# The end of a dense mixture layer: last unit's sums on VectorE, transposes in pairs, raw weights one by one

## The chip, the cores and the metric

The program runs on one core of a Trainium2 chip. The metric is the device time of one execution in microseconds (us), the median of several. The engines named here are TensorE (PE in the profile), VectorE (DVE), ScalarE (ACT), GpSimd (POOL) and SyncE (SP). Each works through its own instructions in order. Transfers are requested on the queues of SyncE and GpSimd.

## The reference, cut to what matters

Attention gives x, 1536 tokens of 512 values. A dense mixture layer follows, with eight experts that all see every token, and then a routed one, in which each token goes to one expert.

```python
def _moe_ref(x, w_gate, w1, w2):          # dense
    P = ...                               # 1536 x 8, normalised eight times
    out = np.zeros((N, D))
    for e in range(E):
        h = np.maximum(x @ w1[e], 0.0)
        out += P[:, e:e + 1] * (h @ w2[e])
    return out

def _moe2_ref(x, w_gate, w_output_gate, w1, w2):   # routed, x is the output above
    logits = x @ w_gate
    e_idx = np.argmax(logits, axis=1)
    gate_w = softmax(logits)[np.arange(N), e_idx]
    eom = 1.0 / (1.0 + np.exp(-(x @ w_output_gate)))
    for e in range(E):
        mask = e_idx == e
        h = np.maximum(x[mask] @ w1[e], 0.0)
        out[mask] = gate_w[mask, None] * eom[mask, e, None] * (h @ w2[e])
    return out
```

## The kernel before

Every float32 product is made of three matmuls of rounded parts (hi and lo): hi times hi, lo times hi, hi times lo. A raw weight tile is loaded, cast to hi on ScalarE (L481, L590) and subtracted to lo on VectorE (L482, L591).

The dense layer goes by half experts hx, 0 to 15. From hx 2 on its tokens are taken in sets of 512 (j), and each set of a half expert is a unit of Strassen's scheme: seven products s1 to s7 for the first layer of this unit, and between them seven products z1 to z7 for the second layer of the unit before. Their order is written out by hand:

```python
TURNS = "s1 z1 s2 z7 z6 s6 s7 z5 s5 z2 z4 s3 z3 s4".split()
```

Half experts up to 13 have three sets, 14 and 15 (the last expert) only two: these are the short ones, and the time in which weights have to be loaded and split is shorter there. The list `later` holds steps (a load, a sum, a split) of which one is taken between products. `load(which, hx, c)` requests one raw quarter of the weights of layer 1 or 2, on SyncE's or GpSimd's queue.

The second layer's results are collected in float32: ScalarE scales a product by the token's gate P (L862), and GpSimd's queue adds it to the sums in DRAM by an accumulating transfer (L867, x2d). `reload` fetches finished sums from x2d into the buffers `acc`.

The four token tiles 8 to 11 of the last expert are left for `rest()`, which ends the dense layer plainly, as half experts P = 16 and R = 17: `mm1_rest` makes the first layer in four blocks c of 12 matmuls of 128x512, `mm2` (in `tile_of`) the second layer for one token tile at a time. The z products of the last unit lie between P's blocks. `done(i)` says that tile i is final.

The routed layer starts inside this stage. `late_steps()` is a second sequence, of which a step is taken between the pieces of the dense one: for each final tile `flip` transposes it on TensorE (four transposes into a bank, a copy to r_xt on ScalarE), and `logits` multiplies it with r_w, the two gating weights side by side. `plain()` begins this phase. `choose`, `totals`, `ranks` and `place` find each token's expert and place, with many small operations on VectorE. The first eight tiles fill two early slots of 128 tokens (`early_*`), and the counts over all tiles (`final_*`) decide the rest. A slot's rows are fetched by an indirect transfer (xg), flipped (flip_x), and multiplied with its expert's weights (whi, wlo); between its two layers the result h is flipped too.

Of the kernel before, what the change touches and what calls it, by code (L numbers as in the profile page):

```python
# [387 lines left out]
class DenseMoe:  # L388
# [65 lines left out]
    def load(self, which, hx, c):  # L454
# [3 lines left out]
        if self.strassen(hx):  # L458
# [7 lines left out]
            (nc.sync if hx == self.FIRST or (which, hx) == (1, self.LAST) else nc.gpsimd).dma_start(  # L466
# [374 lines left out]
    def second(self, hx, j, h):  # L841
# [5 lines left out]
        v, o, *tq = (self.acc(i) for i in (0, 9, 1, 2, 10, 11))  # L847
        t, q = tq[2 * (u % 2):2 * (u % 2) + 2]
# [8 lines left out]
        def add(src, out, th, dh):  # L857

            for c in range(2):
                i = 4 * j + 2 * th + c  # L860
                s = slice(256 * c, 256 * c + 256)
                nc.scalar.activation(  # L862
                    out=out[:, s], in_=src[:, s], func=ACTF.Copy,
                    scale=self.P[:, i, hx // 2:hx // 2 + 1],
                )
# [57 lines left out]
    def steps(self, done, plain):  # L923
# [57 lines left out]
    def pieces(self, done, plain):  # L981
# [9 lines left out]
        waiting, behind = [], None  # L991

# [3 lines left out]
        def new_seconds(hx, n):  # L996
# [28 lines left out]
        for i, (hx, g) in enumerate(units):  # L1025
# [4 lines left out]
            if self.strassen(hx):  # L1030
                self.blocks = {}
                todo = {**self.first(hx, g), **(behind or {})}
                short = hx > self.FULL
                for k, turn in enumerate(self.TURNS):
# [15 lines left out]
                    elif last:  # L1050
                        for what in (self.FIRSTS_LATE if short else self.FIRSTS).get(turn, ()):
                            self.weights(1, n, what)
                    if last and turn == "s4":
                        self.later += [None] + loads(2, n)
                    if g == 0 and behind:
                        if short and turn == "z1":
                            new_seconds(hx, 2)
                        elif short and turn == "z3":
                            new_seconds(hx, 10)
                        elif not short and turn == "z6":  # L1060
                            new_seconds(hx, 0)
# [22 lines left out]
    def rest(self, u, behind, loads, done, plain):  # L1084
# [7 lines left out]
        h = {P: [self.hs[n] for n in (1, 2, 3, 5)], R: [self.hs[n] for n in (0, 4, 1, 2)]}  # L1092

# [7 lines left out]

        self.homes[8] = self.spare
        self.reload((8, 1, 2))
        for c in range(4):
# [151 lines left out]
class Routing:  # L1256
# [8 lines left out]
    def __init__(self, tc, keep, ident, ones, wg, wog, acc, x2d, x2e, psum):  # L1265
        self.tc, self.nc = tc, tc.nc
        self.ident, self.ones, self.acc, self.psum = ident, ones, acc, psum
        self.x2d, self.x2e = x2d, x2e
# [6 lines left out]
        for n, w in (("e", self.EARLY), ("f", self.NS - self.EARLY)):  # L1275
# [6 lines left out]
            })  # L1282
        self.fresh = keep.tile([1, self.NS], I32, name="r_fresh")
# [8 lines left out]
    def begin(self, pool):  # L1292
# [14 lines left out]
        def iota(n, step, base, mult, name):  # L1307
# [928 lines left out]
```

## Time and profile before

| what | value |
|---|---|
| median of 3 runs | 1314.18 us (1314.12 to 1314.45) |
| the profiled execution | 1316.05 us |
| its span on the core | 1314.3 us |
| PE busy | 1281.3 us, 97% |
| DVE busy | 879.2 us, 67% |
| ACT busy | 786.1 us, 60% |
| mean granted clock of TensorE | 0.992 of full |

The profile is of one execution. Its own time is 1.75 us above its span, which is what lies around the program on the core. Times of the trace are counted from the span's start. Attention takes about the first tenth, the dense layer goes on to about 1080 and the routed layer fills the rest.

### The profile page before, as it was taken

The numbers are of one execution on the slowest core, as the hardware profiler recorded it, in microseconds if no ns is written. First come the engines' busy times: TensorE is split into PE (matmuls) and PEld (weight loads), VectorE is DVE, ScalarE is ACT, GpSimd is POOL, SyncE is SP. The second block draws the span as 40 slices with busy tenths as digits, with TensorE's granted clock in tenths as the row PEclk, the third lists the DMA queues.
The fourth block names the chain that finished last, engine by engine and source line by source line (L and its number), as shares of the span: only waits on it lengthen the run. The fifth ranks groups of instructions, "written<-read, shape, count | busy, mean of one in ns | idle before, by whom it ended". The sixth has DMA issues, their size and how long they took to land. (4 is left out here: it accounts for less than half of the span.)

```text
span 1314.3 us, 27146 instructions
## 1 busy us (share of the span) xinstructions
PE 1281.3 (97%) x10227; PEld 1205.4 (92%) x10227; DVE 879.2 (67%) x1712; ACT 786.1 (60%) x1605; POOL 385.3 (29%) x398
## 2 busy tenths in 40 slices
PE   7999999999999999999999999999999998999998
PEld 7888889999999999999999999999999877787886
DVE  6854695877868778777778687787777448514252
ACT  4764322776767667767767676677666525324362
POOL 5652005233424233323334242333222301111110
PEclk8999999999999999999999999999999998999999
DMA  9850237788989798889788897889886668114360
GB/s 215 193 122 10 89 120 273 200 185 182 191 199 207 164 227 169 212 192 195 185 181 196 194 208 166 223 171 210 187 170 151 110 203 288 50 49 153 112 222 22
DMA packets 172828, 223.31 MB, mean 170 GB/s; under 512 B 48079, under 2 KB 102351, under 8 KB 172688
## 3 DMA queue, kind: packets, MB, share of 16 engines
q1 hardware_dynamic: 118448, 145.18, 36.1%
q0 software_dynamic: 54240, 76.30, 33.8%
q8 instruction: 83, 1.36, 0.4%
q14 instruction: 57, 0.47, 0.1%
HBM read 163.76 MB, written 58.46 MB: 169 GB/s over the span
## 5 line engine op out<-in xcount | busy, mean ns | idle before, releaser
L867 POOL DMA_DIRECT2D x2d<-acc x160 | 192.2, 1247 | 514.8 <-ACT acc L862 338.4
L703 PE MATMUL bank<-hi,hhi 128*128 128x256 f32 x748 | 211.5, 283 | 3.5 <-DVE acc L887 1.9
L703 PE MATMUL bank<-hi,hlo 128*128 128x256 f32 x748 | 211.7, 283 | 0.3 <-DVE hlo L738 0.3
L703 PE MATMUL bank<-lo,hhi 128*128 128x256 f32 x748 | 211.6, 283 | 0.0
L703 PE MATMUL bank<-Tlo,hi 128*128 128x256 f32 x640 | 181.0, 283 | 0.0
L703 PE MATMUL bank<-Thi,hi 128*128 128x256 f32 x640 | 180.3, 282 | 0.6 <-ACT t L783 0.6
L703 PE MATMUL bank<-Thi,lo 128*128 128x256 f32 x640 | 180.6, 282 | 0.0
L703 PE MATMUL bank<-hi,acc 128*128 128x256 f32 x744 | 148.0, 282 | 0.7 <-ACT acc L881 0.7
L703 PEld LDWEIGHTS bank<-hi,hhi 128*128 128x128 f32 x748 | 142.5, 190 | 4.4 <-DVE acc L887 2.1
L703 PEld LDWEIGHTS bank<-hi,hlo 128*128 128x128 f32 x748 | 142.1, 190 | 0.5 <-DVE hlo L738 0.5
L703 PEld LDWEIGHTS bank<-lo,hhi 128*128 128x128 f32 x748 | 142.0, 190 | 0.1
L703 PE MATMUL bank<-xhi,hi 128*128 128x256 f32 x480 | 135.4, 282 | 0.7 <-ACT t L797 0.7
L703 PE MATMUL bank<-xlo,hi 128*128 128x256 f32 x480 | 135.4, 282 | 0.0
L703 PE MATMUL bank<-xhi,lo 128*128 128x256 f32 x480 | 135.2, 282 | 0.0
L703 PEld LDWEIGHTS bank<-hi,acc 128*128 128x128 f32 x744 | 121.5, 190 | 0.9 <-ACT acc L881 0.9
L703 PEld LDWEIGHTS bank<-Thi,hi 128*128 128x128 f32 x640 | 121.0, 189 | 1.1 <-ACT t L783 1.0
L703 PEld LDWEIGHTS bank<-Thi,lo 128*128 128x128 f32 x640 | 120.7, 189 | 0.0
L703 PEld LDWEIGHTS bank<-Tlo,hi 128*128 128x128 f32 x640 | 120.3, 188 | 0.0
L738 DVE TENSOR_TENSOR hlo<-t,hhi 128x512 fp32r<-128x512 f32 x160 | 108.0, 687 | 14.5 <-ACT hhi L730 13.5
L730 ACT CAST hhi<-t 128x512 fp32r<-128x512 f32 x160 | 98.1, 621 | 27.4 <-DVE t L832 20.9
L862 ACT ACTIVATE acc<-acc,P 128x256 f32<-128x256 f32 x240 | 107.8, 504 | 5.1 <-DVE acc L904 3.5
L703 PE MATMUL bank<-lo,acc 128*128 128x256 f32 x372 | 105.1, 283 | 0.0
(312 smaller groups left out, 3254.6 us busy)
## 6 DMA issues: line engine op xcount, KB each, us to landing
x2d<-acc POOLq DMA_DIRECT2D x163, 256.0 KB, 5.4
Thi<-td SPq DMA_DIRECT2D x160, 256.0 KB, 3.6
Tlo<-td SPq DMA_DIRECT2D x160, 256.0 KB, 4.6
raw<-in_moe_w_dram POOLq DMA_DIRECT2D x100, 256.0 KB, 5.6
raw<-in_moe_w_dram SPq DMA_DIRECT2D x20, 1024.0 KB, 6.8
raw<-in_moe_w_dram SPq DMA_DIRECT2D x44, 256.0 KB, 4.3
vw<-in_v_dram SPq DMA_DIRECT2D x32, 120.0 KB, 3.6
kn<-in_k_dram SPq DMA_DIRECT2D x8, 384.0 KB, 5.9
```

What stands on the lines that cost most here:

```text
L703: self.nc.tensor.matmul(bank[:, 256 * f:256 * f + 256], x[:, o:o + 128], y[:, k], start=first and n == 1, stop=n == 12, skip_group_check=True,
L730: nc.scalar.copy(hi, src)
L738: nc.vector.tensor_tensor(out=lo, in0=src, in1=hi.bitcast(F32), op=ALU.subtract)
L862: nc.scalar.activation(out=out[:, s], in_=src[:, s], func=ACTF.Copy, scale=self.P[:, i, hx // 2:hx // 2 + 1],)
L867: nc.gpsimd.dma_start(out=self.sums[n:n + 256, 256 * dh:256 * dh + 256].rearrange("(c p) d -> p c d", p=128), in_=out.rearrange("p (c d) - ...
```

## The change

It has four parts. (1) Raw weights of half experts 14 and 15 are all requested on SyncE's queue, one at a time between products, where before most were requested on GpSimd's queue, four together. (2) The products of the last unit (15, second set) are added by VectorE, scaled by P, onto sums that `reload` has fetched into SBUF before; v, t and q live in buffers of T. (3) In `rest()` the last unit's z products and P's blocks lie in another order, the splits and loads around them too, and the first eight tiles are flipped in pairs into two copies (xts), ahead of P's last block. The index patterns are made by GpSimd first and cast by VectorE later (`begin_rest`). (4) x2e, the second scratch copy of the early tiles, is gone, and the steps of the routed layer have other distances.

```diff
@@ -463,7 +463,7 @@
...
-            (nc.sync if hx == self.FIRST or (which, hx) == (1, self.LAST) else nc.gpsimd).dma_start(
+            (nc.sync if hx == self.FIRST or hx > self.FULL else nc.gpsimd).dma_start(
@@ -844,8 +844,13 @@
...
-        v, o, *tq = (self.acc(i) for i in (0, 9, 1, 2, 10, 11))
-        t, q = tq[2 * (u % 2):2 * (u % 2) + 2]
+        final = u + 1 == len(self.sets)
+        if final:
+            v, t, q = (self.t_tile()[0].bitcast(F32) for _ in range(3))
+            o = None
+        else:
+            v, o, *tq = (self.acc(i) for i in (0, 9, 1, 2, 10, 11))
+            t, q = tq[2 * (u % 2):2 * (u % 2) + 2]
         bank = {}
 
@@ -856,6 +861,15 @@
...
 
+            if final:
+                for c in range(2):
+                    i = 4 * j + 2 * th + c
+                    a = self.acc(i)[:, 256 * dh:256 * dh + 256]
+                    nc.vector.scalar_tensor_tensor(
+                        out=a, in0=src[:, 256 * c:256 * c + 256],
+                        scalar=self.P[:, i, hx // 2:hx // 2 + 1], in1=a, op0=ALU.mult, op1=ALU.add,
+                    )
+                return
             for c in range(2):
@@ -938,9 +952,10 @@
...
 
     SECONDS_SOON = (
-        "B11", "sumT1", "sumT3", "T3", "sumT2", "T2", "sumT4", "T1", "B21", "T4", "B22",
+        "B11", None, "sumT1", None, "sumT3", None, "T3", None, "sumT2", 0, "T2", 1, "sumT4", None,
+        "T1", None, "B21", None, "T4", 2, "B22", None, 3,
     )
-    FIRSTS_LATE = {**FIRSTS, "s1": (), "s2": ("A11", "A12"), "z7": ("sumS1",)}
+    FIRSTS_LATE = {**FIRSTS, "s1": ("A11",), "z7": ("sumS1",)}
 
@@ -989,21 +1004,29 @@
...
 
-        def new_seconds(hx, n):
+        def new_seconds(hx):
 
             if hx <= self.FULL:
                 for what in self.SECONDS:
                     self.later += [partial(self.weights, 2, hx, what), None]
                 self.later += [None] + loads(1, hx + 1)
-            elif n == 2:
+            elif hx < self.LAST:
                 for what in self.SECONDS_SOON:
+                    if what is None:
+                        self.later.append(None)
+                    elif isinstance(what, int):
+                        self.later.append(partial(self.load, 1, hx + 1, what))
+                    else:
+                        self.later.append(partial(self.weights, 2, hx, what))
+            else:
+                for what in self.SECONDS:
                     self.later += [partial(self.weights, 2, hx, what), None]
-            elif n == 10:
-                self.later += loads(1, hx + 1)
+                self.later += [None] + loads(1, hx + 1)
 
@@ -1048,17 +1070,17 @@
...
                     elif last:
-                        for what in (self.FIRSTS_LATE if short else self.FIRSTS).get(turn, ()):
+                        for what in (self.FIRSTS_LATE if hx in soon else self.FIRSTS).get(turn, ()):
                             self.weights(1, n, what)
-                    if last and turn == "s4":
+                    if last and hx == self.FULL:
+                        for c in {"s5": (0,), "z3": (1, 2)}.get(turn, ()):
+                            self.load(2, n, c)
+                        if turn == "s4":
+                            self.later += [None, None, partial(self.load, 2, n, 3)]
+                    elif last and turn == "s4":
                         self.later += [None] + loads(2, n)
-                    if g == 0 and behind:
-                        if short and turn == "z1":
-                            new_seconds(hx, 2)
-                        elif short and turn == "z3":
-                            new_seconds(hx, 10)
-                        elif not short and turn == "z6":
-                            new_seconds(hx, 0)
+                    if g == 0 and behind and turn == ("z1" if hx in soon else "z6"):
+                        new_seconds(hx)
                 behind = self.second(hx, g, self.blocks)
                 continue
@@ -1090,6 +1112,10 @@
...
+        space = self.rpool.tile([128, 4, 768], F32, tag="xhi0", name="r_xts").rearrange(
+            "p k n -> p (k n)"
+        )
+        self.xts = [space[:, 512 * n:512 * n + 512] for n in range(2)]
@@ -1099,40 +1125,48 @@
...
+        def seconds(n):
+            for _ in range(n):
+                for _ in behind[order.pop(0)]():
+                    yield u
+
+        self.homes.update({i: self.acc(a) for i, a in ((4, 0), (5, 1), (6, 2), (7, 11))})
         self.homes[8] = self.spare
-        self.reload((8, 1, 2))
+        self.reload((4, 5, 6, 7, 8))
+        yield from seconds(1)
         for c in range(4):
             yield u
             for _ in self.mm1_rest(P, c, h[P][c]):
                 yield u
-            for turn in order[:(2, 3, 2, 0)[c]]:
-                for _ in behind[turn]():
-                    yield u
-            order = order[(2, 3, 2, 0)[c]:]
-            if c == 2:
-                for g in (1, 2):
-                    self.renew(g, F32)
-                self.later += [partial(self.split, 2, P, n) for n in range(4)]
-                self.later += [partial(self.reload, (10, 0, 3, 11, 9, 4, 5, 6, 7))] + loads(1, R)
-                self.later += [partial(done, i) for i in range(8)]
+            yield from seconds((2, 3, 1, 0)[c])
+            if c == 1:
+                a, b = (self.renew(g, F32) for g in (1, 2))
+                self.homes.update({0: a[:, 0], 1: a[:, 1], 2: a[:, 2], 3: b[:, 0]})
+                self.reload((0, 1, 2, 3, 9, 10))
+            elif c == 2:
+                for n in range(4):
+                    self.split(2, P, n)
+                    self.load(1, R, n)
                 plain()
+                for i in range(8):
+                    done(i)
         for t in range(4):
             for _ in tile_of(P, t):
                 yield u + 1
-            if t:
-                self.split(1, R, t - 1)
-                self.load(2, R, t - 1)
+            if t == 0:
+                self.homes.pop(7)
+                self.reload((11,))
+            self.split(1, R, t)
+            self.load(2, R, t)
         for c in range(4):
             yield u + 2
             for _ in self.mm1_rest(R, c, h[R][c]):
                 yield u + 2
-            if c == 0:
-                self.split(1, R, 3)
-                self.load(2, R, 3)
-            else:
-                self.split(2, R, c - 1)
-        self.split(2, R, 3)
-        done("x")
+            if c < 2:
+                self.split(2, R, 2 * c)
+                self.split(2, R, 2 * c + 1)
+            if c == 1:
+                done("x")
         for t in range(4):
@@ -1304,15 +1339,25 @@
...
+    def begin_rest(self):
+
+        pool = self.pool
+        nc, NT, NS, E = self.nc, self.NT, self.NS, self.E
+        for t, ti in self.made:
+            nc.vector.tensor_copy(t, ti)
 
         n = NS - self.EARLY
@@ -1341,25 +1383,26 @@
...
-        if i < self.TILES:
-            self.nc.sync.dma_start(out=self.x2e[rows, :], in_=self.acc(i))
-        else:
+        if i >= 4:
             self.nc.gpsimd.dma_start(out=self.x2d[rows, :], in_=self.acc(i))
...
-    def flip(self, i):
+    def flip(self, i, xt=None):
         nc = self.nc
         tr = self.psum("a", [128, 4, 128])
         x = self.acc(i)
         for k in range(4):
             nc.tensor.transpose(tr[:, k], x[:, 128 * k:128 * k + 128], self.ident)
-        xt = self.pool.tile([128, 4, 128], F32, tag="r_xt", name="r_xt", bufs=1)
+        if xt is None:
+            xt = self.pool.tile([128, 512], F32, tag="r_xt", name="r_xt", bufs=1)
+        xt = xt.rearrange("p (k n) -> p k n", k=4)
         nc.scalar.copy(xt, tr)
-        self.xt = xt
+        self.xt[i] = xt
 
     def logits(self, i):
         ps = self.psum("b", [128, 2 * self.E])
+        xt = self.xt.pop(i)
         for k in range(4):
-            self.nc.tensor.matmul(ps, self.xt[:, k], self.w[:, k], start=(k == 0), stop=(k == 3))
+            self.nc.tensor.matmul(ps, xt[:, k], self.w[:, k], start=(k == 0), stop=(k == 3))
         self.nc.vector.tensor_copy(self.lg[:, i], ps)
 
@@ -2012,7 +2054,7 @@
...
-        "routed": {"a": (4,), "b": (5,), "t": (0, 1), "m2": (3, 2), "m1": (6, 7)},
+        "routed": {"a": (4, 0), "b": (5,), "t": (0, 1), "m2": (3, 2), "m1": (6, 7)},
@@ -2125,8 +2167,7 @@
...
 
-            def tiles(i, n, first, w):
-                yield from wait(first)
@@ -2136,7 +2177,19 @@
...
-            yield from tiles(0, T, 4, 2)
+            while 0 not in finished:
+                yield
+            for j in range(T):
+                routing.flip(j, moe.xts[j % 2])
+                if j:
+                    routing.logits(j - 1)
+                if j % 2:
+                    yield
+                if j == 3:
+                    routing.begin_rest()
+            routing.logits(T - 1)
+            routing.choose(0, T)
+            yield from wait(6)
             routing.totals(T)
             routing.ranks(0, T)
```

What stands in each engine's order is shown at three places. The first is SyncE's queue at the end of the dense layer; `raw` from L471 are second-layer weights of P, `raw` from L474 first-layer weights of R, `acc` and `spare` fetched sums. Before:

```order
L657 DMA acc_107<-x2d 128x512 x2
L471 DMA raw<-in_moe_w_dram 128x512 x4
L1297 DMA r_w<-in_moe_w_gate_dram 128x4x8
L1297 DMA r_w<-in_moe_w_output_gate_dram 128x4x8
L657 DMA acc_110<-x2d 128x512
L657 DMA acc_107<-x2d 128x512
L657 DMA acc_13512<-x2d 128x512
L657 DMA acc_110<-x2d 128x512 x2
L657 DMA acc_13512<-x2d 128x512 x2
L657 DMA acc_13513<-x2d 128x512 x2
L474 DMA raw<-in_moe_w_dram 128x4x128 x4
```

With the change:

```order
L657 DMA acc_106<-x2d 128x512 x3
L657 DMA acc_109<-x2d 128x512
L657 DMA spare<-x2d 128x512
L471 DMA raw<-in_moe_w_dram 128x512 x4
L657 DMA acc_13485<-x2d 128x512 x3
L657 DMA acc_13486<-x2d 128x512
L657 DMA acc_109<-x2d 128x512 x2
L474 DMA raw<-in_moe_w_dram 128x4x128 x4
L1332 DMA r_w<-in_moe_w_gate_dram 128x4x8
L1332 DMA r_w<-in_moe_w_output_gate_dram 128x4x8
L657 DMA acc_109<-x2d 128x512
```

The two requests of r_w stood right behind P's raw weights; now they stand behind eleven fetched sums in all and behind R's four raw loads.

The second place is VectorE at the end of P's first layer; `lo` from L482 are the split parts of P's second-layer weights, `r_lg` (L1363, now L1406) the copies of the logits. Before:

```order
L689 SCALAR_TENSOR_TENSOR hlo<-bank_13460,hhi 128x512
L904 TENSOR_TENSOR acc_110<-bank_13390,acc_110 128x512
L1311 CAST r_ilo<-r_iota 128x128
L1311 CAST r_ihi<-r_iota 128x20
L1319 CAST r_ihalf<-r_ihi 1x18
...
L1311 CAST r_tok<-r_iota 128x12
L1311 CAST r_desc<-r_iota 128x8
...
L1340 MEMSET r_fresh 1x2
L482 TENSOR_TENSOR lo_13565<-raw,hi_13564 128x512
...
L482 TENSOR_TENSOR lo_13587<-raw,hi_13586 128x512
```

With the change (L868 is the addition of a product onto a fetched sum):

```order
L868 SCALAR_TENSOR_TENSOR acc_109<-Thi,P,acc_109 128x256
L689 SCALAR_TENSOR_TENSOR hlo<-bank_13493,hhi 128x512
L868 SCALAR_TENSOR_TENSOR acc_106<-bank_13355,P,acc_106 128x256 x2
L482 TENSOR_TENSOR lo_13525<-raw,hi_13524 128x512
...
L482 TENSOR_TENSOR lo_13543<-raw,hi_13542 128x512
L1406 COPY r_lg<-bank_13593 128x16
...
L1406 COPY r_lg<-bank_13621 128x16
L1360 CAST r_ilo<-r_iota 128x128
L1360 CAST r_ihi<-r_iota 128x20
```

The casts of the index patterns stood ahead of the four splits and now stand behind the first logits; the splits now stand directly behind the last unit's last sums.

The third place is TensorE at slot 0 of the routed layer: the matmuls of L1411, L1405 and L1406 (now L1454, L1448, L1449) form the totals and ranks of all tiles, L1886 (now L1929) flips h, and L1857 (now L1900) multiplies. Before:

```order
L1848 MATMUL bank_14252<-ident,xg 128x128 x4
L1362 MATMUL bank_14261<-r_w,r_xt 128x16 x4
L1886 MATMUL bank_14284<-ident,h 128x128 x4
L1886 MATMUL bank_14293<-ident,h 128x128 x4
L1857 MATMUL bank_14302<-whi_13558,ht0hi 128x512
...
L1857 MATMUL bank_14302<-whi_13558,ht0lo 128x512
L1411 MATMUL bank_14312<-r_run,ones 128x8
L1405 MATMUL bank_14314<-r_oh,r_upper 128x32
L1406 MATMUL bank_14314<-r_run,ones 128x32
L1857 MATMUL bank_14302<-whi_13558,ht0hi 128x512
```

With the change:

```order
L1900 MATMUL bank_14251<-wlo_13950,xthi 128x512
L1900 MATMUL bank_14251<-whi_13949,xtlo 128x512
L1454 MATMUL bank_14265<-r_run,ones 128x8
L1448 MATMUL bank_14267<-r_oh,r_upper 128x32
L1449 MATMUL bank_14267<-r_run,ones 128x32
L1891 MATMUL bank_14365<-ident,xg 128x128 x4
L1929 MATMUL bank_14374<-ident,h 128x128 x4
...
L1929 MATMUL bank_14383<-ident,h 128x128 x4
L1900 MATMUL bank_14392<-whi_13571,ht0hi 128x512
```

The totals stood behind both flips of h and nine matmuls of slot 0's second layer; now they stand ahead of both flips, and between them and the flips stands only the flip of the second slot's rows.

## Rows read from the trace of the kernel before

**Rows 1.** Table by stretches: us, busy PE, PEld, DVE, ACT, POOL, PEclk, DMA share, GB/s.

```profile
940.00:960.00 20.00, 19.07 (x158) 18.66 (x157) 15.34 (x25) 14.17 (x29) 6.09 (x7) 1.00 0.87 214
960.00:980.00 20.00, 18.07 (x146) 17.74 (x145) 15.73 (x26) 13.83 (x28) 3.57 (x4) 0.97 0.83 189
980.00:1000.00 20.00, 18.74 (x146) 18.33 (x145) 13.89 (x23) 11.42 (x24) 6.92 (x8) 0.94 0.83 174
...
1020.00:1040.00 20.00, 19.32 (x140) 18.15 (x139) 12.23 (x20) 11.88 (x24) 4.77 (x4) 1.00 0.71 131
1040.00:1060.00 20.00, 16.56 (x85) 13.83 (x84) 7.91 (x21) 7.37 (x16) 5.95 (x10) 0.91 0.76 151
...
1080.00:1100.00 20.00, 18.93 (x92) 15.21 (x91) 18.18 (x72) 8.09 (x13) 3.28 (x4) 1.00 0.63 216
1100.00:1120.00 20.00, 15.98 (x80) 13.59 (x80) 12.31 (x15) 10.86 (x14) 1.08 (x2) 0.83 0.85 296
1120.00:1140.00 20.00, 18.34 (x108) 15.23 (x106) 14.58 (x68) 9.02 (x16) 1.63 (x2) 1.00 0.04 15
...
1280.00:1300.00 20.00, 20.00 (x95) 16.34 (x94) 6.91 (x8) 8.04 (x12) 1.01 (x1) 1.00 0.05 18
```

**Rows 2.** Timeline of TensorE: start, duration, line, operation, count [idle before, releaser].

```profile
973.04 0.28 PE L703 MATMUL bank<-Thi,hi 128*128 128x256 f32 x1
...
974.48 0.28 PE L703 MATMUL bank<-hi,hhi 128*128 128x256 f32 x1
...
978.00 0.39 PE L703 MATMUL bank<-hi,hhi 128*128 128x256 f32 x1 [1.93 <-DVE acc L887]
...
1046.51 0.39 PE L682 MATMUL bank<-xhi,hi 128*128 128x512 f32 x1
...
1049.28 0.39 PE L631 MATMUL bank<-hi,hhi 128*128 128x512 f32 x1
...
1053.10 0.50 PE L631 MATMUL bank<-lo,hhi 128*128 128x512 f32 x1 [3.44 <-DVE lo L482]
...
1062.52 0.96 PE L1362 MATMUL bank<-r_w,r_xt 128*128 128x16 f32 x8
...
1063.33 0.64 PE L1354 MATMUL bank<-ident,acc 128*128 128x128 f32 x4
...
1063.72 0.48 PE L631 MATMUL bank<-hi,hhi 128*128 128x512 f32 x1
...
1109.00 1.89 PE L1362 MATMUL bank<-r_w,r_xt 128*128 128x16 f32 x8 [4.02 <-ACT r_xt L1356]
```

**Rows 3.** Timeline of ScalarE: casts of raw weights, dense (L590), then routed (L1821).

```profile
994.14 0.62 ACT L590 CAST hi<-raw 128x512 fp32r<-128x512 f32 x1 [3.15 <-DMA raw<-in_moe_w_dram]
...
1106.47 1.99 ACT L1821 CAST whi<-raw 128x1024 fp32r<-128x1024 f32 x2 [2.17 <-DMA raw<-in_moe_w_dram]
```

**Rows 4.** Timeline of GpSimd with its queue: raw loads of the last short expert.

```profile
988.09 3.36 POOL L466 DMA_DIRECT2D raw<-in_moe_w_dram  x4
```

**Rows 5.** Timeline of VectorE: around the split of P's weights, and the final routing chain.

```profile
1050.44 0.23 DVE L1311 CAST r_ilo<-r_iota 128x128 f32<-128x128 int32 x1 [4.47 <-POOL r_iota L1309]
...
1052.36 0.69 DVE L482 TENSOR_TENSOR lo<-raw,hi 128x512 fp32r<-128x512 f32 x1
...
1052.96 1.89 DVE L482 TENSOR_TENSOR lo<-raw,hi 128x512 fp32r<-128x512 f32 x3
...
1126.81 0.17 DVE L1466 TENSOR_SCALAR r_ni<-bank 128x8 int32<-128x8 f32 x1 [1.52 <-PE bank L1411]
...
1133.13 2.33 DVE L1824 TENSOR_TENSOR wlo<-raw,whi 128x1024 fp32r<-128x1024 f32 x2
```

**Rows 6.** Timeline of SyncE's queue: the two requests of the gating weights (r_w).

```profile
1036.58 0.43 SPq L1297 DMA_DIRECT2D r_w<-in_moe_w_gate_dram  x1
1037.06 0.50 SPq L1297 DMA_DIRECT2D r_w<-n_moe_w_output_gate_dram  x1
```

**Rows 7.** Line view of L1297, the same two requests: time to landing.

```profile
DMA to landing us min/median/max: 4.4/4.5/4.7
```

More of the change, by code (lines that the diff above doesn't have):

```diff
@@ L991, in pieces @@
         waiting, behind = [], None
+        soon = range(self.FULL + 1, self.LAST)
         def loads(which, hx):
             return [partial(self.load, which, hx, c) for c in range(4)]
-        def new_seconds(hx, n):
+        def new_seconds(hx):
             if hx <= self.FULL:
@@ L1032, in pieces @@
                 todo = {**self.first(hx, g), **(behind or {})}
-                short = hx > self.FULL
                 for k, turn in enumerate(self.TURNS):
@@ L1050, in pieces @@
                     elif last:
-                        for what in (self.FIRSTS_LATE if short else self.FIRSTS).get(turn, ()):
+                        for what in (self.FIRSTS_LATE if hx in soon else self.FIRSTS).get(turn, ()):
                             self.weights(1, n, what)
-                    if last and turn == "s4":
-                        self.later += [None] + loads(2, n)
-                    if g == 0 and behind:
-                        if short and turn == "z1":
-                            new_seconds(hx, 2)
-                        elif short and turn == "z3":
-                            new_seconds(hx, 10)
-                        elif not short and turn == "z6":
-                            new_seconds(hx, 0)
+                    if last and hx == self.FULL:
[4 more added lines that the diff above has]
+                    elif last and turn == "s4":
+                        self.later += [None] + loads(2, n)
+                    if g == 0 and behind and turn == ("z1" if hx in soon else "z6"):
+                        new_seconds(hx)
                 behind = self.second(hx, g, self.blocks)
@@ L1263, with __init__ @@
     EARLY, TILES = 2, 8
-    def __init__(self, tc, keep, ident, ones, wg, wog, acc, x2d, x2e, psum):
+    def __init__(self, tc, keep, ident, ones, wg, wog, acc, x2d, psum):
         self.tc, self.nc = tc, tc.nc
         self.ident, self.ones, self.acc, self.psum = ident, ones, acc, psum
-        self.x2d, self.x2e = x2d, x2e
+        self.x2d = x2d
         self.wg, self.wog = wg, wog
@@ L1282, in __init__ @@
             })
+        self.xt = {}
         self.fresh = keep.tile([1, self.NS], I32, name="r_fresh")
@@ L1305, in begin, with iota @@
         )
-        def iota(n, step, base, mult, name):
-            ti = pool.tile([128, 128], I32, tag="r_ohhi", name="r_iota", bufs=1)
-            nc.gpsimd.iota(ti[:, 0:n], pattern=[[step, n]], base=base, channel_multiplier=mult)
-            t = pool.tile([128, n], F32, name=name)
-            nc.vector.tensor_copy(t, ti[:, 0:n])
-            return t
-        self.i_lo = iota(128, 1, 0, 0, "r_ilo")
-        self.i_hi = iota(NS, 1, 0, 0, "r_ihi")
+        def iota(n, step, base, mult, name, tag):
+            ti = pool.tile([128, n], I32, tag=tag, name="r_iota", bufs=1)
+            nc.gpsimd.iota(ti, pattern=[[step, n]], base=base, channel_multiplier=mult)
+            return pool.tile([128, n], F32, name=name), ti
+        made = [
+            iota(128, 1, 0, 0, "r_ilo", "r_ohhi"), iota(NS, 1, 0, 0, "r_ihi", "r_le"),
+            iota(NT, 128, -2048, 1, "r_tok", "r_val"), iota(E, -1, E, 0, "r_desc", "r_ptg"),
+        ]
+        self.i_lo, self.i_hi, self.tok, self.desc = (t for t, _ in made)
+        self.lg = pool.tile([128, NT, 2 * E], F32, name="r_lg")
+        self.made = made
+    def begin_rest(self):
[3 more added lines that the diff above has]
+            nc.vector.tensor_copy(t, ti)
         n = NS - self.EARLY
@@ L1327, in begin @@
         )
-        self.tok = iota(NT, 128, -2048, 1, "r_tok")
-        self.desc = iota(E, -1, E, 0, "r_desc")
         self.unit = pool.tile([128, E], F32, name="r_unit")
         nc.vector.memset(self.unit, 1.0)
-        self.lg = pool.tile([128, NT, 2 * E], F32, name="r_lg")
         self.oh = pool.tile([128, NT, E], F32, name="r_oh")
@@ L1830, in gather @@
         self.nc.gpsimd.indirect_dma_start(
-            out=xg, out_offset=None, in_=self.r.x2e if s < self.r.EARLY else self.r.x2d,
+            out=xg, out_offset=None, in_=self.r.x2d,
             in_offset=bass.IndirectOffsetOnAxis(ap=self.r.of("gidx", s), axis=0),
@@ L2000 @@
     x2d = dram.tile([N, DM], F32, name="x2d")
-    x2e = dram.tile([128 * Routing.TILES, DM], F32, name="x2e")
     td = dram.tile([N // 512, 2, 4, 128, 512], F32, name="td")
@@ L2073 @@
         routing = Routing(
-            tc, const, ident, ones, moe2_w_gate, moe2_w_output_gate, acc, x2d, x2e, psum
+            tc, const, ident, ones, moe2_w_gate, moe2_w_output_gate, acc, x2d, psum
         )
@@ L2126, in wait, with tiles @@
                     yield
-            def tiles(i, n, first, w):
-                yield from wait(first)
+            def tiles(i, n, w):
                 for j in range(i, i + n):
@@ L2159, in late_steps @@
                 moe2.gather(s)
-            yield from wait(3)
             moe2.split(0, 1)
@@ L2163, in late_steps @@
             moe2.split(0, 1)
-            yield from wait(6)
+            yield from wait(4)
             moe2.flip_x(0)
-            yield from wait(3)
+            yield from wait(4)
             moe2.split(0, 1)
-            yield from wait(6)
+            yield from wait(5)
             moe2.split(0, 1)
             finished.add("early")
-            yield from tiles(T, NT - T, 0, 2)
+            yield from tiles(T, NT - T, 2)
             routing.totals(NT)
```

## The prediction

> **What bounds the kernel now.** I read the table by stretches first, then TensorE's timeline around each hole, then the other engines' timelines at the same moments. In the table [rows 1] the reader is to see that TensorE is full nearly everywhere (20.00 of 20 us in the last stretch shown) at granted clock 1.00, so a microsecond lost on TensorE moves the end by a microsecond. Holes stand only where the change works: the two short experts (940 to 1000) and the closing stage, from 1027 on. Idle time there is 20 minus PE's busy time: 0.93, 1.93 and 1.26 in the short experts, and 0.68, 3.44, 1.07, 4.02 and 1.66 in the five closing stretches shown. To that comes the low clock: a mean of 0.97 over 20 us is 1.2 us at the lower level (1.2 GHz for 2.4), which costs 0.6; 0.94 costs 1.2, 0.91 costs 1.8 and 0.83 costs 3.4. Together 5.9 us in the short experts and 16.1 in the closing stage. This is the lower figure. Counted from start to start of neighbouring matmuls, against the spacing of undisturbed ones, I get 7 and 18.8, because the matmuls beside a wait are stretched too (those at 978.00 and 1053.10 [rows 2]). I use 7.0 and 18.8: 25.8 us is all that this change can win.
>
> Who is late: in the short experts ScalarE, whose casts of raw weights wait up to 3.15 us for the transfer (994.14 [rows 3]). It was requested on GpSimd's queue, four pieces in one burst of 3.36 us starting at 988.09 [rows 4], behind the accumulating transfers of that queue. In the closing stage there are two large holes. The second layer's first matmul group waits 3.44 us at 1053.10 for its split weights (L482) [rows 2]; VectorE had waited 4.47 us for GpSimd's index pattern (r_iota) just ahead of them [rows 5]. And at 1109.00 the logits wait 4.02 us for a copy on ScalarE [rows 2], which there stood behind a cast of expert weights that had itself waited 2.17 us for its transfer (1106.47 [rows 3]).
>
> **The change part by part.**
>
> *Raw weights one by one on SyncE's queue.* They no longer stand behind accumulates, and are asked for up to ten microseconds earlier. All waits of the short experts should go: 7.0 gained, so the closing stage starts at T = 1027.3 - 7.0 = 1020.3. Bounds: 0 if SyncE's own fetches of T hold them as long, 7.0 if not; I take the upper end, since the slots in SyncE's order lie 3 us or more ahead of the casts. Every one of these requests now delays the T fetches behind it by about 0.4 us (by r_w's requests, the nearest row, 0.43 and 0.50 [rows 6]); these are asked for a product or more ahead and hide it.
>
> A sentence of the Trainium skill speaks against this part ("DMA: Bandwidth & Descriptors", section "Issuing engines are not separate DMA queues"): transfers of all issuers share the same sixteen engines, and spreading them over issuers saves only the time of issuing. By it alone the gain would be the few tenths by which one issue is shorter, and the whole sum 7 us worse. Rows 4 show why I don't follow it here: what is late is the request, not the transfer.
>
> *Last unit's products added on VectorE into sums fetched ahead.* It takes the accumulating transfers, their landing and the fetch behind them off the end of the unit. ScalarE's scalings go; VectorE gets two 128x256 additions a product. One product of 12 matmuls takes 1.44 us (973.04 to 974.48 [rows 2]), one of P's first-layer blocks 2.77 (1046.51 to 1049.28). Seven products and three blocks end at T + 10.1 + 8.3 = T + 18.4, and one product waits for a sum on VectorE, about 0.25 (bounds 0 and the 0.69 of one such VectorE operation [rows 5]). So T + 18.6.
>
> *Eight transposes in pairs, logits behind them.* TensorE does two flips (0.39 each with its gap, 1063.33 to 1063.72 [rows 2]) and then wants the first logits, at T + 19.3. They need r_w, the gating weights. The order shows r_w moved on SyncE: before it was requested right after P's raw weights, now behind R's four raw loads, each of which waits until VectorE has split the P weights (four L482). These stand behind the last sums: z3's two additions end at T + 19.6 (no row; between 0 and two times 0.6 after z3), then 0.69 and three more in 1.89 [rows 5], T + 22.1; the last raw load goes out in 0.4; r_w's two requests at T + 22.55 and 23.05 [rows 6] take 4.4 to 4.7 us to land [rows 7]: T + 27.4. TensorE idles from 19.3 to 27.4: **8.2 us**, and nothing covers it, because P's last block stands behind the logits in TensorE's order. Lower bound: if r_w were there, ScalarE's flip copy, behind four casts, would end near T + 20.8, a wait of 1.5.
>
> The Trainium skill puts the fixed cost of a transfer at about 2 us ("DMA: Bandwidth & Descriptors", section "Latency and other measured facts"). By it the hole would be 5.7 us rather than 8.2; r_w's own rows [rows 7] show more than twice that, and the measured value stands.
>
> *The clock behind the hole.* After an idle stretch the trace shows the lower level for a while: [rows 1] give 3.6 us of it in the stretch with the 3.44 idle, 6.8 us in the one with the 4.02. What follows here is light work, six flips, eight logits (0.81 each, 1062.52 to 1063.33; such a group of eight matmuls lasts 0.96 at the full clock and 1.89 at the lower, at 1109.00 [rows 2]) and one block: 2.3 + 6.5 + 2.8 = 11.6 us at full clock. Bounds: 1.8 (as after 3.44 idle) to 11.6 (all of it at half). I take 5.
>
> *Second layer of P.* Its fourth tile wants the bank that VectorE frees only behind the early routing chain, some 25 small operations (0.14 each, as in the next part) and one large, 4 us; most lies beside two tiles' matmuls, 1.15 stays (0 to 4). Four small waits (r_run, a flip's bank, the gathered rows, the first slot's split) are 0.2 to 0.7 each, together 1.6 (0 to 3).
>
> *Final counts ahead of the slot's flips.* In before the three small matmuls of the final totals stood nine matmuls into slot 0's second layer, so VectorE's chain lay beside matmuls. Now they stand ahead of the flips of h, and VectorE does the chain (46 small operations, 1126.81 to 1133.13, 6.3 us [rows 5]) ahead of the xtlo that frees the bank of the second h flip. TensorE has only two flips to do meanwhile: 6.3 + 0.6 + 0.3 - 0.7 = **6.5**, and some 0.1 for handing on: 6.6. Bounds: 4.5 if the chain packs tighter, 8.9 if the two wlo operations ahead of it (2.33 together [rows 5]) are not done. The clock behind it: 1.7 (0.8 to 3.4, [rows 1]).
>
> *Gone with it*: the iota wait, the ScalarE copy behind late expert loads (they are now requested earlier in the order, ahead of three of R's raw loads), the second scratch copy: all in the 18.8.
>
> **Sum.** Against the profiled execution's own 1316.05: -25.8 + 0.25 + 8.2 + 5.0 + 1.15 + 1.6 + 6.6 + 1.7 = -1.3, or 1314.8. The median of the runs is 1.87 below the profiled one, so 1313. By the lower figure of the gain, 22.0, it would be 1316.7 for the median.
>
> **Rivals.**
>
> A, the forecast: both new waits come as worked out and eat the gain. 1309 to 1317, by the bounds of the waits and of the clock.
>
> B, one of the two is not there: r_w lands before the flips (SyncE's raw loads don't wait as I read them), or VectorE's chain finishes under other work. For it: the waits are read from an order, and VectorE has room, with 7.91 and 12.31 us of work in the 20 us from 1040 and from 1100 [rows 1]. Against: both engines work in order. Without the r_w hole but with ScalarE's 1.5, 6.7 less, and the clock with it up to 5: 1301 to 1306. Without the chain's wait, 8.3 less: 1305.
>
> C, slower: the clock stays at the lower level through all of the flips and logits. It costs 11.6 instead of 5, 1320, and it decides as soon as more than 9 us of that stage run at half. For it: flips and logits are much lighter than the 128x512 groups that followed the holes of before. Against: in before the level came back within 7 us although flips and logits stood in it.
>
> D, the change doesn't do what it says in the short experts: SyncE, in order, holds raw loads behind T fetches that wait for a free buffer, and they land as late as before. Against: GpSimd's burst alone takes 3.36 us [rows 4]. Half to all of the 7 is missing: 1316 to 1320. The rule of the Trainium skill named above would end here too.
>
> **How the numbers follow.** A 45%, B 25%, C 20%, D 10%. The likeliest gives 1313. The bound of what can be told from no change is 0.2%, 2.6 us. Faster than 1311.6 takes a third of A and all of B: 0.40. Between 1311.6 and 1316.8 lies the larger part of A and half of D: 0.33. Slower: C, the other half of D and a little of A: 0.27. The range reaches from the middle of B to beyond C's centre, 1303 to 1321; A's own is 1309 to 1317.
>
> **What would show it.** In the profile after: no wait of ScalarE on raw between the short units; TensorE's first logits after the dense layer with 8 us of idle time ahead, released by the DMA of r_w; a granted clock well below 1 in the 12 us behind; a second wait of 6 to 7 us at the second flip of h, released by VectorE's xtlo; no wait on the P split or on r_xt. The forecast is wrong if r_w's request starts before T + 15, if the second h flip waits less than 3 us, or if the short experts keep more than 3 us of idle time.

## The result, and the profile after

| kernel | median | runs | ratio to the kernel before | TensorE's path | granted clock |
|---|---|---|---|---|---|
| before | 1314.15 us | 1311.67 to 1315.87 | | 1079.97 us | 0.992 |
| changed | 1325.55 us | 1324.19 to 1328.42 | 1.0092 [1.0078, 1.0107] | 1088.75 us | 0.979 |

The change costs 11.4 us; 1313 and a range of 1303 to 1321 were forecast. The last columns are of the profiled executions. "TensorE's path" is the time from the first matmul with T (the first Strassen unit) to the start of the last matmul. It leaves out the first 230 us, which differ by up to 4.4 us between executions (the first T matmul stands between 225.88 and 230.26 in the profiles shown here), and what follows the last matmul. Here and below a ratio compares the means of the runs, its bracket is a 95% interval, and one run of 3721 us (r_w early) is left out of it.

The table by stretches of the changed kernel, columns as in [rows 1]:

```profile
940.00:960.00 20.00, 20.00 (x170) 20.00 (x169) 17.84 (x30) 16.29 (x33) 4.87 (x5) 1.00 0.89 221
960.00:980.00 20.00, 20.00 (x169) 20.00 (x169) 16.91 (x28) 14.29 (x29) 4.83 (x4) 1.00 0.85 178
980.00:1000.00 20.00, 20.00 (x170) 20.00 (x169) 16.04 (x27) 15.49 (x31) 5.31 (x5) 1.00 0.82 184
...
1020.00:1040.00 20.00, 18.32 (x120) 16.45 (x118) 13.10 (x24) 7.99 (x15) 4.14 (x11) 1.00 0.84 235
1040.00:1060.00 20.00, 11.58 (x49) 10.81 (x50) 2.26 (x16) 1.76 (x3) 0.50 (x1) 0.57 0.33 97
1060.00:1080.00 20.00, 20.00 (x80) 17.80 (x81) 6.49 (x29) 4.77 (x10) 0.00 (x0) 0.58 0.07 18
1080.00:1100.00 20.00, 19.77 (x96) 16.06 (x94) 16.84 (x54) 8.24 (x12) 2.90 (x2) 1.00 0.64 225
...
1120.00:1140.00 20.00, 13.02 (x60) 10.41 (x59) 16.41 (x67) 7.99 (x13) 0.10 (x1) 0.74 0.16 53
```

The short experts (first three rows) have no idle time and the full clock; that is the gain that was forecast. From 1040 on stand two rows at a clock of 0.57 and 0.58, then one hole at 1120. TensorE's timeline shows the two places:

```profile
1037.29 1.04 PE L1394 MATMUL bank<-ident,acc 128*128 128x128 f32 x8
1048.42 1.86 PE L1405 MATMUL bank<-r_w,r_xts 128*128 128x16 f32 x8 [10.10 <-DMA r_w<-n_moe_w_output_gate_dram]
...
1071.99 0.77 PE L631 MATMUL bank<-hi,hhi 128*128 128x512 f32 x1
1072.56 0.63 PE L631 MATMUL bank<-lo,hhi 128*128 128x512 f32 x1
...
1076.83 0.47 PE L631 MATMUL bank<-hi,hlo 128*128 128x512 f32 x1
1077.13 0.39 PE L631 MATMUL bank<-hi,hhi 128*128 128x512 f32 x1
...
1122.13 0.36 PE L1454 MATMUL bank<-r_run,ones 128*128 128x8 f32 x2 [0.44 <-DVE r_run L1433]
...
1124.49 0.86 PE L1929 MATMUL bank<-ident,h 128*128 128x128 f32 x4 [1.06 <-DVE r_r L1486]
...
1130.83 1.11 PE L1929 MATMUL bank<-ident,h 128*128 128x128 f32 x4 [5.48 <-DVE xtlo L1884]
```

Both flips are done by 1038.3, then the first logits wait 10.10 us for r_w, and when they start they run at the lower level (1.86 us for eight matmuls, against 0.96 in [rows 2]). P's second layer starts at 1071.99 with 0.43 from matmul to matmul, and the full spacing of 0.23 is back at 1077.13 only. At 1122 to 1131 the other hole: 0.44, 1.06 and 5.48 us around the final totals and the flips of h. SyncE's queue and the line view of r_w say why the first hole is there:

```profile
1038.99 3.09 SPq L474 DMA_DIRECT2D raw<-in_moe_w_dram  x4
1042.13 0.61 SPq L1332 DMA_DIRECT2D r_w<-in_moe_w_gate_dram  x1
1042.79 0.90 SPq L1332 DMA_DIRECT2D r_w<-n_moe_w_output_gate_dram  x1
```

```profile
DMA to landing us min/median/max: 5.5/5.7/6.0
```

R's raw loads went out from 1038.99 to 1042.08, r_w behind them, and it took 5.5 to 6.0 us to land, where the same requests took 4.4 to 4.7 before [rows 7]. Part of that belongs to the execution: in the four later profiles with r_w at the same place it took from 4.3 to 5.8. On VectorE stand ahead of them the last sums and the four splits; and further down, two wlo operations and the chain of the final counts ahead of xtlo:

```profile
1037.49 0.88 DVE L868 SCALAR_TENSOR_TENSOR acc<-bank,P,acc 128x256 f32<-128x256 f32 x2
1038.28 2.49 DVE L482 TENSOR_TENSOR lo<-raw,hi 128x512 fp32r<-128x512 f32 x4
...
1121.91 2.36 DVE L1867 TENSOR_TENSOR wlo<-raw,whi 128x1024 fp32r<-128x1024 f32 x2
1124.18 0.16 DVE L1509 TENSOR_SCALAR r_ni<-bank 128x8 int32<-128x8 f32 x1
...
1130.04 0.13 DVE L1738 TENSOR_SCALAR r_used<-r_endsf 1x1 int32<-1x1 f32 x1
1130.10 0.67 DVE L1884 TENSOR_TENSOR xtlo<-bank,xthi 128x512 fp32r<-128x512 f32 x1
```

### The profile page after: what moved, and what is told of

Read it like the earlier page. It is cut to its first block, busy times and chain, and to the rows that moved or that the text cites. A ratio compares the mean times of both kernels' runs of the same rounds, so it can differ in the third digit from the quotient of the medians.

```text
span 1323.6 us, 27132 instructions
## 1 busy us (share of the span) xinstructions
PE 1287.5 (97%) x10227; PEld 1213.7 (92%) x10227; DVE 882.6 (67%) x1720; ACT 782.9 (59%) x1597; POOL 377.8 (29%) x386
## 5 line engine op out<-in xcount | busy, mean ns | idle before, releaser
L881 POOL DMA_DIRECT2D x2d<-acc x156 | 189.2, 1257 | 500.5 <-ACT acc L876 317.7
L876 ACT ACTIVATE acc<-acc,P 128x256 f32<-128x256 f32 x234 | 105.1, 504 | 1.9 <-DVE acc L918 1.9
```

Of the source, the lines that this page charges most:

```text
L876: nc.scalar.activation(out=out[:, s], in_=src[:, s], func=ACTF.Copy, scale=self.P[:, i, hx // 2:hx // 2 + 1],)
L881: nc.gpsimd.dma_start(out=self.sums[n:n + 256, 256 * dh:256 * dh + 256].rearrange("(c p) d -> p c d", p=128), in_=out.rearrange("p (c d) - ...
```

## The experiments

The path in each run is that of its one profile, the median that of all its runs. The diffs are cut to the lines that matter.

### r_w early

```diff
+        done("w")                      # rest(), ahead of the first reload: requests r_w
         self.homes.update({i: self.acc(a) for i, a in ((4, 0), (5, 1), (6, 2), (7, 11))})
```

> The changed kernel, with the two requests of r_w at the head of the closing stage on SyncE's queue instead of behind R's raw loads. Theory H (the 10.1 us hole in front of the first logits puts TensorE at its lower clock, and the light work behind keeps it there): the hole shrinks to about 1.5 (ScalarE's flip copies stand behind four casts) and the clock stays full, so 8.6 and 14.6 us go: about 1302, granted clock 1.00 in the flips. Rival L (the flips and logits are so light that the clock falls without any hole): only the hole's 8.6 go, about 1317, and the clock of that stage stays near 0.57.

Measured: 1305.80 us, ratio 0.9958 [0.9930, 0.9987], path 1067.56. Stretches, the two TensorE rows of the first flips and logits, and the landing of r_w (the trace has it for one of the two requests):

```profile
1020.00:1040.00 20.00, 19.81 (x132) 17.93 (x130) 13.08 (x24) 8.29 (x17) 3.49 (x9) 1.00 0.89 236
1040.00:1060.00 20.00, 19.27 (x131) 17.30 (x132) 10.26 (x52) 7.70 (x16) 1.99 (x4) 1.00 0.40 122
```

```profile
1038.77 1.04 PE L1398 MATMUL bank<-ident,acc 128*128 128x128 f32 x8
...
1040.73 1.06 PE L1409 MATMUL bank<-r_w,r_xts 128*128 128x16 f32 x8 [0.92 <-ACT r_xts L1402]
```

```profile
DMA to landing us min/median/max: 2.7/2.7/2.7
```

In the profiled execution the hole is 0.92 us, the clock 1.00 in both stretches, and the stage from the first logits to P's second layer lasts 12.8 us (1040.73 to 1053.50) instead of 23.6 (1048.42 to 1071.99). 19.8 us come back in the median, 21.2 on the path; the 9.2 by which the hole shrank are less than half. Theory L, by which the light work lowers the clock by itself, gave 1317 and does not fit this trace.

The runs fall into two groups, though: six took 1302 to 1306 us at a granted clock of 0.992 to 0.995, and three took 1315 to 1316 us at 0.983. No trace of the three is kept. Their clock is 0.009 lower over some 1304 us, which is an estimated 23 us more at the lower level, about as long as the low stretch that the runs with part of the hole filled show below. So a wait of 0.92 us did not keep the clock in every execution.

### The hole filled with matmuls

```diff
                 routing.flip(j, moe.xts[j % 2])
+                if j == 1:
+                    moe.fill(44)       # 44 matmuls of 128x512 into two free banks, read by nobody
                 if j:
                     routing.logits(j - 1)
```

> The changed kernel, with 44 matmuls of 128x512 (10.1 us at the full clock) between the second flip and the first logits, whose results nobody reads: the hole keeps its length, but TensorE is not idle in it. Theory H: the clock stays at its full level through flips, logits and P's last block, and 14.6 us go: about 1311. Rival L: the clock falls in the light work all the same: about 1325.

Measured: 1312.12 us, ratio 0.9993 [0.9980, 1.0007], path 1076.46. Stretches:

```profile
1040.00:1060.00 20.00, 20.00 (x129) 17.41 (x127) 3.27 (x20) 3.69 (x7) 0.99 (x2) 1.00 0.35 106
1060.00:1080.00 20.00, 19.38 (x92) 15.92 (x92) 16.03 (x68) 4.93 (x11) 0.00 (x0) 1.00 0.52 172
```

TensorE is just as late at the first logits (1048.76), but not idle, and the flips and logits behind run at 1.00, 12.75 us to P's second layer. 13.4 us come back with the hole as long as ever: this is the price of the clock alone. All ten runs lie between 1311 and 1316 us at a clock of 0.992 to 0.994, so without idle time the light work never brought the low stretch, and theory L is out.

### Half of the hole filled, and three quarters

The same with 22 and with 34 matmuls.

> As the run with 44 unread matmuls in the hole, with 22: TensorE works through the first 5 us of it and is idle for the other 5. If any hole of about this length ahead of the light flips and logits costs the lower clock until the dense matmuls of P's second layer, the stage stays at half the clock and the time is that of the changed kernel, about 1325. Rival (the price grows with the length of the hole): about 1318.

> The same with 34 unread matmuls: 2.5 us stay idle. In the kernel before, an idle time of 1.93 us ahead of dense matmuls was followed by 3.3 us of the lower clock. If the light work behind decides how long the low clock lasts, some of the 14.6 us comes back here too: 1318 to 1325. If so short a hole is harmless: 1312, as with 44.

Measured: 1325.10 us, 1.0087 [1.0061, 1.0113], path 1086.66, with 22; 1325.20 us, 1.0086 [1.0061, 1.0112], path 1086.32, with 34. The idle time left was 4.24 and 2.08 us. With 34, the stretches and the logits:

```profile
1040.00:1050.00 10.00, 7.92 (x40) 6.39 (x39) 1.15 (x3) 0.00 (x0) 0.70 (x2) 1.00 0.68 200
1050.00:1060.00 10.00, 10.00 (x53) 9.60 (x51) 1.50 (x14) 2.35 (x4) 0.00 (x0) 0.56 0.00 0
1060.00:1070.00 10.00, 10.00 (x41) 9.22 (x42) 1.70 (x7) 2.28 (x4) 0.00 (x0) 0.50 0.11 28
1070.00:1080.00 10.00, 10.00 (x38) 8.10 (x37) 6.90 (x43) 1.90 (x5) 0.00 (x0) 0.74 0.08 26
```

```profile
1048.33 1.04 PE L1414 MATMUL bank<-r_w,r_xts 128*128 128x16 f32 x8 [2.08 <-DMA r_w<-n_moe_w_output_gate_dram]
...
1050.42 0.96 PE L1414 MATMUL bank<-r_w,r_xts 128*128 128x16 f32 x8
...
1052.11 1.73 PE L1414 MATMUL bank<-r_w,r_xts 128*128 128x16 f32 x8
```

After 2.08 us of idle time the first logits still run at the full clock, and about 3 us later the level falls (1.73 for eight matmuls); it stays down until 1075, in P's second layer. So the price does not grow with the hole: 4.24 or 2.08 us idle cost nearly what 10.1 did, and 0.92 (r_w early) cost none of the clock in the profiled execution. The theory of a hole of 2 us being harmless here falls, and so does the idea that half the wait costs half.

### The final totals later

```diff
             yield from tiles(T, NT - T, 2)
+            yield from wait(4)
             routing.totals(NT)
```

> The changed kernel, with the final totals and ranks four steps later, behind the flips of h and six matmuls of slot 0's second layer. If the wait of 6.6 us at the flips of h comes from VectorE's chain of small operations standing ahead of them, it goes, and with it most of the low clock behind it (2.6): about 1317 to 1319. Rival: the chain only delays the expert weights instead, and the same wait comes back some 10 us later: 1325.

Measured: 1320.09 us, ratio 1.0054 [1.0037, 1.0071], path 1080.34. TensorE's timeline there:

```profile
1121.87 0.60 PE L1929 MATMUL bank<-ident,h 128*128 128x128 f32 x4
...
1124.81 0.66 PE L1929 MATMUL bank<-ident,h 128*128 128x128 f32 x4 [2.35 <-DVE xtlo L1884]
1125.22 0.49 PE L1900 MATMUL bank<-whi,ht0hi 128*128 128x512 f32 x1
```

```profile
1120.00:1140.00 20.00, 17.65 (x99) 14.94 (x99) 16.79 (x69) 8.28 (x15) 1.52 (x2) 1.00 0.18 66
```

The two waits at the flips of h, 6.5 us, became one of 2.35: xtlo now stands behind VectorE's wlo operations only. 5.5 us come back in the median, 1 us less than forecast, and 8.4 on the path of the profiled execution, the fastest of the four. Of these 8.4, 1.0 lies at r_w, whose hole was 9.1 us in this profile. Nothing of it came back as a wait further down.

The 2.35 us here are as long as the hole that cost some 24 us of low clock above. But behind them stand one flip and then 128x512 matmuls one after the other, and the granted clock of the stretch is 1.00.

### Both moves, and the splits later

```diff
             yield u
-            for _ in self.mm1_rest(P, c, h[P][c]):
+            for n, _ in enumerate(self.mm1_rest(P, c, h[P][c])):
                 yield u
+                if c == 3:
+                    self.split(2, P, n)
+                    self.load(1, R, n)
```

(The fourth stands behind the loop, and the loop over the four at c == 2 is gone.) The first run has the two moves above alone; the second has them and this edit.

> The changed kernel with both moves of the first and second experiment: r_w's requests at the head of the closing stage, and the final totals behind the flips of h. If the two holes are independent, their effects add: 1305.8 less the 5.5 that the later totals brought alone, about 1300. Rival (the second hole only hid behind the first, or VectorE's chain becomes late for the expert weights): 1305.

> As the run with both moves, and the four splits of P's second-layer weights with R's raw loads one by one between the groups of P's last block, so that ScalarE's copies of the first flips stand ahead of the four casts. The 0.9 us wait of the logits on ScalarE goes: 1 us below the run with both moves. Rival: the last split comes too late for P's second layer, and TensorE waits about 2 us there: 1 us above it.

Measured: 1300.35 us, ratio 0.9912 [0.9885, 0.9940], path 1063.52, for both moves; 1298.82 us, 0.9878 [0.9858, 0.9899], path 1061.81, with the splits later. The two holes are independent, their effects add (19.8 and 5.5 from 1325.55 give 1300.3). With the splits later the logits wait only 0.2 us for ScalarE, and no wait for the last split appears. The stretch around the flips of h with both moves, then waits and stretches of the last kernel:

```profile
1100.00:1120.00 20.00, 17.65 (x83) 14.75 (x81) 14.54 (x55) 6.95 (x12) 3.99 (x1) 0.83 0.15 57
```

```profile
PE bank L1936 <- DVE xtlo L1891: 2.3, 1, 2.3
PE bank L631 <- DVE acc L643: 0.9, 1, 0.9
PE bank L1936 <- ACT h L1923: 0.3, 1, 0.3
PE bank L1412 <- ACT r_xts L1405: 0.2, 1, 0.2
```

```profile
1040.00:1060.00 20.00, 19.65 (x134) 17.22 (x132) 10.69 (x50) 9.42 (x19) 2.23 (x4) 1.00 0.39 120
1100.00:1120.00 20.00, 17.66 (x90) 14.82 (x88) 16.75 (x68) 8.62 (x14) 1.17 (x1) 0.91 0.20 66
```

This one is the fastest, 1.2% below the kernel before. How much of the last 1.5 us the splits brought is not shown: the intervals overlap, 0.7 us went at the logits, and the profiles also differ in the clock around the flips of h. The wait there is the same, 2.35 and 2.34 us, but the clock of the stretch is 0.83 in one and 0.91 in the other. By the prediction's arithmetic that is 6.8 and 3.6 us at the lower level, at a cost of 3.4 and 1.8. One of the six runs with both moves took 1310 us at a clock of 0.985, as three did with r_w early; of the five with the splits later none did.

### The first part alone, and before once more

The first part of the change (queue, SECONDS_SOON, FIRSTS_LATE and the loads between products) was put into the kernel before; it ran a second time in a later group, beside the kernel before unchanged.

> The kernel before with the first part of the change alone, the raw weights of the short experts one by one on SyncE's queue. If the 7 us that the short experts lost came from the requests standing behind accumulating transfers on GpSimd's queue, they go: about 1307, no wait of TensorE between 940 and 1000. Rival (issuers share the transfer engines, so only the time of issuing is saved): about 1314.

> The kernel before with the first part of the change alone, once more: its trace shows TensorE 7.1 us earlier at the start of the closing stage, its runs only 1.9 us less in the median. If the rest is spread between executions (the first 230 us and the last scatter differ by up to 4 and 2 us between profiles), the median comes nearer to 1307 and the start of the closing stage is again 7 us nearer to the end of attention. If the loss belongs to the kernel, the median stays at 1312.

> The kernel before, unchanged: a second profile of it beside the first. If the spread of the first 230 us and of the last 2 us lies between executions, they differ here from the first profile's 228.25 us to the first Strassen product and 6.1 us from the last matmul to the end, and the closing stage between does not. The time: 1314.

Measured: 1312.09 us, 0.9985 [0.9972, 0.9999], path 1072.63; 1310.76 us, 0.9974 [0.9961, 0.9988], path 1075.24; before again 1314.81 us, 1.0006 [0.9991, 1.0021], path 1079.47. The first run's stretches, and its requests of the raw weights that were late in [rows 3]:

```profile
940.00:960.00 20.00, 20.00 (x170) 20.00 (x169) 17.80 (x29) 15.20 (x30) 4.21 (x5) 1.00 0.90 220
960.00:980.00 20.00, 20.00 (x169) 20.00 (x168) 17.06 (x29) 15.59 (x31) 5.22 (x5) 1.00 0.82 182
980.00:1000.00 20.00, 20.00 (x170) 20.00 (x169) 15.90 (x27) 14.42 (x29) 4.71 (x5) 1.00 0.87 189
```

```profile
983.18 2.92 SPq L466 DMA_DIRECT2D raw<-in_moe_w_dram  x4
```

No idle time between 940 and 1000, and no wait of ScalarE for a raw transfer; the kernel is unchanged behind that. The requests start at 983.18 where they started at 988.09 [rows 4]. The edit moves them to another queue and to an earlier place together, so it does not show which of the two was needed. From the first T matmul to P's first block the two profiles need 791.95 and 792.19 us, the kernel before 799.05 and, in its second profile, 797.07. So 5 to 7 us are gained there, as the kernel before loses a different amount each time: ScalarE's wait for the last raw weights was 3.15 in its first profile [rows 3] and 2.57 in its second:

```profile
990.73 0.62 ACT L590 CAST hi<-raw 128x512 fp32r<-128x512 f32 x1 [2.57 <-DMA raw<-in_moe_w_dram]
```

The median shows only 1.9 and 3.7 of it, and the 1307 that was expected is not reached. About 2 us go behind the last matmul: from its start to the end of the span pass 6.1 us in both profiles of the kernel before, and 7.9 to 8.3 in all those with the first part, the changed kernel too. Why is open: no engine's row shows it.

## Why the prediction was wrong

*Right.* The short experts: their idle time and ScalarE's waits for raw transfers are gone, and the gain is there, 7.1 against the first profile, 5 against the second (7.0 forecast). The rule of the Trainium skill ("DMA: Bandwidth & Descriptors", section "Issuing engines are not separate DMA queues"), that issuers share the transfer engines, did not decide here: with the first part alone the path fell by 4 to 7 us, with requests that also went out earlier. The r_w hole came at its place, with its cause, 10.10 us for 8.2; the wait at the flips of h came as 6.5 us in two pieces, for 6.6. Waits on the P split and on r_xt are gone.

*The step that failed* is the term "the clock behind the hole": 5 us taken between bounds of 1.8 and 11.6. It was 13.1, in a stage that lasts 12.8 at the full clock: 10.8 in the flips, logits and block (23.6 less 12.8), and 2.3 in the first tile of P's second layer (1071.99 to 1077.13 is 5.1 us for twelve matmuls, which take 2.9 at the full clock in the run with r_w early). The run with the filled hole puts it at 13.4. The text took the 3.6 and 6.8 us of low clock in [rows 1] as if the level returned after a time. Both stretches ended in an unbroken row of 128x512 matmuls. Of the second, behind the logits at 1109.00 [rows 2], TensorE's timeline before shows it: nine matmuls, and the logits behind them run at the full level again (0.96):

```profile
1111.47 0.78 PE L1857 MATMUL bank<-whi,xthi 128*128 128x512 f32 x1
...
1115.04 0.58 PE L1857 MATMUL bank<-whi,xtlo 128*128 128x512 f32 x1
1115.46 0.96 PE L1362 MATMUL bank<-r_w,r_xt 128*128 128x16 f32 x8
```

With the change only threes of them (P's last block) stand between the flips and logits until P's second layer. So the argument against rival C, that the level had come back "although flips and logits stood in it", passed over what else stood there. The upper bound too was too low, because it ended with the light stage, and the level came back 5 us later. This is rival C, which had 20% and 1320; its price of 11.6 was 1.5 too low. That an unbroken row set earlier would have ended the low stretch earlier is not tested.

*Smaller misses.* r_w landed 1 us later than its row of before and behind raw loads of 0.77 us each, not 0.4: +1.9. The low clock at the flips of h (0.74 over 20 us, about half of it idle) took about 2.2 rather than 1.7, against the spacing of the same rows with the totals later. The prediction has no term for the 2.0 us behind the last matmul. Against that, the small waits and the bank's wait, 2.75 together in the sum, were 0.9. 1.9 + 8.1 + 0.5 + 2.0 - 1.85 = 10.65. The profiled execution (1325.47) missed the sum's 1314.8 by 10.7, with a first part that was 1.45 us shorter than in the profile the sum started from: 12.1 to explain, of which 1.5 is left in pieces that I did not assign.

## What to carry to other kernels

A wait ahead of light TensorE work is priced by the work behind it more than by its own length. Ahead of the flips and logits, 2 us of idle time cost the clock nearly as much as 10, and the bill was nearly the doubled time of everything up to the next dense matmuls, and 2 us more in these. Ahead of a dense group, 2.35 us cost nothing in one profile and an estimated 1.8 and 3.4 us in two others. So look at what follows a new wait before pricing it, and take the bound to the next dense stage. A small load that a stage begins with belongs at the head of the queue: behind four larger loads that each wait for a buffer, 32 KB decided 20 us in the median. Even the 0.9 us that were left seem to have brought the low stretch in three runs of nine, so a wait there is worth removing whole. And when a chain on VectorE moves past a wait of TensorE, count whose bank it frees.

## What the runs showed of the hardware

The granted clock fell 3 us after a 2.08 us idle time had ended, in the middle of light work, and stayed at the lower level for some 24 us; with matmuls in place of the idle time the same light work kept the full clock, 1.00 over 20 us. The requests of r_w took 2.6 to 2.8 us to land when they were sent early (three profiles, one of the two requests in each), 4.1 to 5.0 right behind P's four raw loads (four profiles of the kernel before, two of them with the first part of the change), and 4.3 to 6.0 right behind R's four (five profiles). The Trainium skill gives about 2 us as the fixed cost of a transfer ("DMA: Bandwidth & Descriptors", section "Latency and other measured facts"). The first of these is near it, the longest is three times it.
